# Attention loads paced by a 4-byte transfer, and the zero fills of expert 0's rows moved to later tiles

## The chip, the cores and the metric

The kernel runs on one core of a Trainium2 chip. The metric is device time in microseconds (us) for one execution, as the median of several runs. Beside the runs there is one profiled execution, and all rows of the trace below come from it; their times count from the first instruction of the span.

## The reference

Three layers follow each other on 2304 tokens (4 sequences of 576) of width 512. The first is a retention attention with 8 heads of 64, with no softmax: `scores = q k^T / 8`, multiplied by a decay mask, then `scores v`.

```
ret = scale * (q @ k^T) * Dmat          # Dmat = gamma_h ** (i - j) for i >= j, else 0
x = (ret @ v) laid out as 2304 x 512
noisy = x @ w_gate + log1p(exp(x @ w_noise)) * noise     # 8 experts, the best 2 per token
out[token] += weight * (relu(x[token] @ w1[e]) @ w2[e])  # F = 1024
h = out @ w_in;  g = h * clip(h + 3, 0, 6) / 6;  result = g @ w_out   # 2048 wide
```

## The kernel before

The work is written in one fixed order, and each engine runs its own part of it as an in-order queue. The attention stage takes 18 tiles of 128 tokens. Tile t needs three loads of 256 KB each (`load`, line 190: k, q, v), which SyncE's queue (SP) issues. VectorE scales k (`ks`, line 195) and q (`qs`, line 200), TensorE transposes k (`tr`) and multiplies (`qk`, line 225), and VectorE multiplies the scores by the mask into the tile `pt` (line 227, two instructions per tile). `av` and `av2` then use `pt` (lines 239 and 249), `kv` updates the running state (line 281).

In iteration t of the loop in `attention` (line 470) the program first issues `load(t + 3)`, for t from 1 to 14, and in four of the iterations (`WL`) a load of expert weights (`w_load`, lines 557 and 559). Then come, for the tile before, the row form of x (`xt`, evicted by ScalarE at line 295 into a buffer of the pool `row`) and `zero(t - 1)`; then `tr(t + 2)`, `av(t)`, `av2(t)`, `kv(t)`, `ks(t + 3)`, `qs(t + 3)` and `qk(t + 1)`. Tiles 0 to 3 are loaded ahead of the loop. k, q, v, `pt` and the weights share a pool of 32 buffers (`big`), handed out in turn as older ones come free; the program's order and these buffers are all that holds a load back.

After every third tile the router (`route`) works in small steps through the next two iterations and gives each token of the three tiles two slots in the DRAM array `xe`, one region per expert. `send` then scatters rows: GpSimd (POOL) first copies or clears a 4-byte `spacer` (lines 413 and 411), which waits for the engine that just produced a given tile, and then issues an indirect DMA of 128 rows of 2 KB (line 414). There are three sends in an iteration while slots are waiting: six scatters for a group of three tiles. Scatters are declared not to depend on each other. The groups are called 1 to 6 here; the scatters of group 1 are scatter 1 to 6.

`zero` writes 128 rows of zeros (`self.warm`, a buffer of the pool `row`) into expert 0's region, so that rows that no token fills are defined. The four fills cover rows 0 to 128, 128 to 256, 232 to 360 and 488 to 616. The framework orders any two DMAs that write overlapping parts of `xe`, and a scatter counts as writing all of it.

In iteration 14 (`GA`) the program sends all that is left of the first 12 tiles (four groups, 24 scatters) and issues `x_load(0, 0)` (line 670), three loads of expert 0's rows from `xe` behind these scatters, and behind them a 4-byte transfer into the DRAM word `paced` (line 514). These rows are turned at line 704, in the last iteration, and feed the first expert. The pool `row` has 13 buffers, of which the first four are `warm`, two state tiles and a table.

Of the kernel before, what the change touches and what calls it, by code (L numbers as in the profile page):

```python
# [19 lines left out]
NT = N // 128  # L20
RA, RB = 120, 128
NA, NB = 3 * RA, 2 * RB
CAP = NA + NB
# [10 lines left out]
P = 128  # L34
# [44 lines left out]
class K:  # L79
# [90 lines left out]

    def zero(self, j):

        if j < 4:
            r = (P, 2 * P, NA, CAP)[j]
            self.nc.gpsimd.dma_start(self.xe[r - P:r], self.warm.bitcast(F32))

    def load(self, t, names="kqv"):
# [36 lines left out]
    def qk(self, t):  # L214
        nc = self.nc
        r = self.raw[t]
        mk = C_MM if t % 9 == 4 else C_MK
        mask = self.c[:, mk:mk + P]
        pt = self.big([P, 2, 4, P])
        p0 = self.ps.tile([P, 4, P], F32, name="sc0", tag="ga")  # L220
        p1 = self.ps.tile([P, 4, P], F32, name="sc1", tag="gb")
        for a in range(4):
            for s, p in enumerate((p0, p1)):
                h = slice(s * 64, s * 64 + 64)
                nc.tensor.matmul(p[:, a, :], r["kT"][h, a, :], r["qT"][h, a, :], start=True, stop=True)  # L225
        for s, p in enumerate((p0, p1)):
            nc.vector.tensor_mul(pt[:, s], p, mask[:, None, :].to_broadcast([P, 4, P]))
        r["pt"] = pt
# [210 lines left out]
        yield  # L439

    def attention(self):
        self.raw, self.xrow, self.sq = {}, {}, []
        self.consts()
        self.load(0, "kq")
        self.load(1, "kq")
        self.nc.sync.dma_start(self.c[:, C_MK:], self.i["cst"][:, C_MK:C_W])
        self.load(0, "v")
        self.load(2, "kq")
        self.load(1, "v")
        self.load(3, "kq")  # L450
        self.load(2, "v")
        self.load(3, "v")
        self.busy(BZ[0])
        self.table()
        self.ks(0)
        self.tr(0)
        self.qs(0)
        self.ks(1)
        self.qs(1)
        self.busy(BZ[1])  # L460
        self.qk(0)
        self.gate_w()
        self.tr(1)
        self.ks(2)
        self.qs(2)
        self.late_consts()
        groups = [(g, 3) for g in range(0, NT, 3)]
        assert EARLY in [g[0] for g in groups]
        self.live, self.sent, self.xg = [], 0, {}
        for t in range(NT):  # L470
            if 0 < t < NT - 3:
                self.load(t + 3)
            if t in WL:
                self.w_load()
            self.rstep()

            if t:
                self.xt(t - 1)
                self.zero(t - 1)
            if 0 < t < NT - 2:  # L480
                self.tr(t + 2)
            if t and t % 3 == 0:
                self.gate(t - 1, groups)
            self.rstep()
            self.av(t)
            self.rstep()
            self.wstep(WM)

            self.av2(t)
            self.kv(t)  # L490
            if t == 0:
                self.tr(2)
            if t + 1 == NT:
                xs = self.x_new(0)
                self.x_tile(0, xs, 0, "acc")
                self.x_tile(0, xs, 1, "gb")
            self.rstep()
            if t + 3 < NT:
                self.ks(t + 3)
                self.qs(t + 3)  # L500

            if t + 1 < NT:
                self.qk(t + 1)
            if t % 3 == 2 and t + 1 < NT:
                self.gsum(t // 3)
            if t + 1 < NT:
                self.rstep()
            if t == GA:
                while self.sent < EARLY:
                    self.rstep()  # L510
                    self.send()
                self.xr = {}
                self.x_load(0, 0)
                self.nc.sync.dma_start(self.paced, self.xr[0, 0, 2][0:1, 0:1])
            if t in WS:
                self.w_split()
            if t + 1 < NT:
                self.wstep(WN)
        self.gsum(NT // 3 - 1)
        self.x_tile(0, xs, 2, "tp")  # L520
        self.xt(NT - 1)
        self.gate(NT - 1, groups)
        self.rstep()
        self.wstep(WN)
        return xs
# [913 lines left out]
```

## Time and profile before

| | |
|---|---|
| Median of 3 runs | 935.56 us (934.23 to 936.85) |
| Profiled execution, its own time | 936.64 us |
| Its span, first to last instruction | 934.5 us, so 2.14 us lie around it |
| TensorE busy | 921.8 us, 99% of the span |
| VectorE, ScalarE, GpSimd busy | 606.8, 466.5 and 235.9 us |
| Granted TensorE clock, mean | 0.998 |
| DMA | 221.22 MB, 237 GB/s over the span |

PE is the matmul side of TensorE and PEld its weight-load side; DVE is VectorE, ACT ScalarE, POOL GpSimd, SPq the queue of SyncE. Ends of matmuls are modelled, so a gap is easier to see on PEld than on PE. A "DMA share" is the mean busy share of the core's 16 DMA engines in a stretch; packets in flight overlap, so it can read slightly above 1. Brackets behind a row give the idle time of the engine before it, and what ended it.

### The profile page before, as it was taken

To read this page: it belongs to the slowest core of one execution; us is meant where nothing else is said; L and a number is where in the kernel's file an instruction comes from. 1 tells how busy PE (TensorE), PEld (TensorE's weight loads), DVE (VectorE), ACT (ScalarE), POOL (GpSimd) and SP (SyncE) were. 2 spreads that over 40 slices of the span, in tenths; PEclk is the share of its full clock that TensorE was granted. 3 is DMA by queue.
4 is the path that set the end of the run, shared out by engine and by line. 5 is a ranking of instruction groups with operands and counts; after the bars stand their busy time and mean duration, and the time that the engine had idled before them with its cause. 6 is when DMAs were issued, how large, how long until landed. Compare 5 with 4: busy or idle time off the path is not lost.

```text
span 934.5 us, 17789 instructions
## 1 busy us (share of the span) xinstructions
PE 921.8 (99%) x6314; PEld 818.2 (88%) x6314; DVE 606.8 (65%) x1327; ACT 466.5 (50%) x1025; POOL 235.9 (25%) x324
## 2 busy tenths in 40 slices
PE   9999999999999999999999999999999999999996
PEld 6887888988988889888888899999889998999985
DVE  5787747878879797787847446545745554564442
ACT  4666435455564645545544445544554464455432
POOL 1345531324233242432400221042004113300000
PEclk9999999999999999999999999999999999999999
DMA  9964877859879688896636787877578676846541
GB/s 339 386 243 147 304 243 232 238 187 280 259 241 282 227 256 271 248 267 218 224 111 214 265 298 252 307 247 240 188 262 270 205 258 227 271 166 228 167 150 49
DMA packets 123742, 221.22 MB, mean 237 GB/s; under 512 B 13037, under 2 KB 60915, under 8 KB 123643
## 3 DMA queue, kind: packets, MB, share of 16 engines
q1 hardware_dynamic: 113819, 190.47, 61.9%
q0 software_dynamic: 9392, 28.73, 9.1%
q8 instruction: 52, 0.85, 0.4%
q10 hardware_dynamic: 432, 0.79, 0.2%
q14 instruction: 47, 0.39, 0.1%
HBM read 163.97 MB, written 55.97 MB: 235 GB/s over the span
## 4 chain that ended last, share of the span: by engine, by line
PE 86%; DVE 7%; DMA 3%; issue 1%; ACT 1%; POOL 1%; SPq 0%; DVEq 0%; ACTq 0%; POOLq 0%
PE p L754 39%; PE ga L737 12%; PE gb L737 9%; PE mga L1168 7%; PE p L1168 5%; PE mgb L1168 2%; PE mtp L1168 2%; PE sc L225 2%; DVE b L591 1%; PE px L249 1%; PE p L293 1%; DVE cvt L635 1%; PE p L209 1%; DMA xe<-s,free 1%; DVE h L796 1%
## 5 line engine op out<-in xcount | busy, mean ns | idle before, releaser
L754 PE MATMUL p<-b,h 128*120 128x512 f32 (+1 forms) x1056 | 260.9, 395 | 0.0
L754 PEld LDWEIGHTS p<-b,h 128*120 128x120 f32 (+1 forms) x1056 | 189.2, 185 | 41.4 <-DVE h L796 0.4
L754 PE MATMUL p<-b,b 128*128 128x512 f32 x768 | 180.0, 390 | 0.0
L754 PEld LDWEIGHTS p<-b,b 128*128 128x128 f32 x768 | 142.3, 188 | 28.2
L737 PE MATMUL ga<-x,b 128*128 128x360 f32 (+1 forms) x768 | 134.4, 324 | 2.9 <-DVE h L796 2.9
L737 PEld LDWEIGHTS ga<-x,b 128*128 128x128 f32 x768 | 124.6, 188 | 12.1 <-DVE h L796 7.7
L640 POOL TENSOR_TENSOR cvl<-cvl,cvs 128x256 f32<-128x256 f32 x64 | 50.3, 785 | 229.9 <-ACT cva L621 163.0
L591 DVE TENSOR_TENSOR b<-b,b 128x512 fp32r<-128x512 f32 x128 | 89.6, 734 | 13.2 <-ACT b L590 12.9
L737 PE MATMUL gb<-b,b 128*128 128x256 f32 x672 | 89.7, 283 | 0.0
L737 PEld LDWEIGHTS gb<-b,b 128*128 128x128 f32 x672 | 86.9, 190 | 1.2
L885 POOL DMA_INDIRECT s<-yd,slotc x36 | 36.4, 1011 | 166.9 <-DVE x L991 48.4
L590 ACT ACTIVATE b<-b 128x512 fp32r<-128x512 f32 x128 | 74.1, 626 | 0.0
L1206 DVE SCALAR_TENSOR_TENSOR b<-s,b 128x512 fp32r<-128x512 f32 x64 | 44.3, 693 | 44.9 <-ACT b L1205 42.0
L1205 ACT ACTIVATE b<-s 128x512 fp32r<-128x512 f32 x64 | 40.5, 632 | 59.3 <-DVE s L1203 56.8
L796 DVE SCALAR_TENSOR_TENSOR h<-gb,h 128x256 fp32r<-128x256 f32 (+1 forms) x64 | 27.7, 433 | 50.2 <-PE p L754 35.2
L641 POOL TENSOR_TENSOR cvl<-cvt,cvl 128x256 f32<-128x256 f32 x64 | 58.2, 909 | 5.0
L1202 ACT ACTIVATE s<-s,three 128x512 f32<-128x512 f32 x64 | 45.9, 717 | 24.8 <-DVE s L1189 23.2
L1168 PE MATMUL mga<-b,b 128*128 128x256 f32 x384 | 56.3, 283 | 0.0
L1189 DVE TENSOR_TENSOR s<-p,mc 128x256 f32<-128x256 f32 x32 | 13.6, 424 | 65.4 <-PE p L1168 60.1
L1168 PEld LDWEIGHTS mga<-b,b 128*128 128x128 f32 x384 | 52.6, 191 | 2.5
L1203 DVE SCALAR_TENSOR_TENSOR s<-s,s 128x512 f32<-128x512 f32 x64 | 44.0, 687 | 7.5 <-DMA paced<-s 4.9
L1173 ACT ACTIVATE mc<-mga 128x256 f32<-128x256 f32 x64 | 24.6, 384 | 48.2 <-PE mga L1168 48.0
(206 smaller groups left out, 1433.6 us busy)
## 6 DMA issues: line engine op xcount, KB each, us to landing
b<-wc SPq DMA_DIRECT2D x112, 512.0 KB
b<-in_moe_w_dram SPq DMA_DIRECT2D x64, 512.0 KB
wc<-b SPq DMA_DIRECT2D x32, 512.0 KB
s<-xe SPq DMA_DIRECT2D x140, 64.0 KB
s<-in_moe_w_in_dram SPq DMA_DIRECT2D x32, 256.0 KB
s<-in_moe_w_out_dram SPq DMA_DIRECT2D x32, 256.0 KB
b<-wc SPq DMA_DIRECT2D x32, 256.0 KB
yd<-s SPq DMA_DIRECT2D x24, 240.0 KB
```

The costliest lines, as they stand in the source:

```text
L590: self.nc.scalar.activation(h, a, AF.Copy)
L591: rest = lambda h=h, l=l, a=a: self.nc.vector.tensor_sub(l, a, h.bitcast(F32))
L640: nc.gpsimd.tensor_mul(lf, lf, s.bitcast(F32))
L641: nc.gpsimd.tensor_add(lf, t.bitcast(F32), lf)
L737: nc.tensor.matmul(p, a[k], b[:, k, :n], start=(i == 0), stop=(i == 11))
L754: nc.tensor.matmul(a[:R], x[:, c], y[:, fi, :], start=(first and i == 0), stop=(last and i == 2))
L796: nc.vector.scalar_tensor_tensor(hl, p, 0.0, hh.bitcast(F32), op0=OP.max, op1=OP.subtract)
L1168: nc.tensor.matmul(t, w[:, u, k], x[:, z, k], start=(first and i == 0), stop=(last and i == 5), skip_group_check=True)
L1202: nc.scalar.activation(r, x, AF.Relu, bias=self.three)
L1203: v.scalar_tensor_tensor(x, r, 6.0, x, op0=OP.min, op1=OP.mult)
L1205: nc.scalar.activation(h[:, 0], x, AF.Copy, scale=1.0 / 6.0)
L1206: v.scalar_tensor_tensor(h[:, 1], x, 1.0 / 6.0, h[:, 0].bitcast(F32), op0=OP.mult, op1=OP.subtract)
```

## The change

Two things are changed. First, from iteration 3 on, a transfer of 4 bytes from the tile `pt` of tile t - 1 to the DRAM word `paced` is put into SP's queue ahead of `load(t + 3)`. It can only be issued once VectorE has written that part of `pt`. Each `qk(t)` for t from 2 to 13 keeps its `pt` for it. Second, `zero` does its four fills for j = 3, 4, 5, 6 in place of 0, 1, 2, 3, that is in iterations 4 to 7 in place of 1 to 4; the rows of the four fills and their order are the same.

```diff
     def zero(self, j):
 
-        if j < 4:
-            r = (P, 2 * P, NA, CAP)[j]
+        if 2 < j < 7:
+            r = (P, 2 * P, NA, CAP)[j - 3]
             self.nc.gpsimd.dma_start(self.xe[r - P:r], self.warm.bitcast(F32))
...
         pt = self.big([P, 2, 4, P])
+        if 1 < t < NT - 4:
+            self.pts[t] = pt
...
-        self.raw, self.xrow, self.sq = {}, {}, []
+        self.raw, self.xrow, self.sq, self.pts = {}, {}, [], {}
...
             if 0 < t < NT - 3:
+                if t > 2:
+                    self.nc.sync.dma_start(self.paced, self.pts.pop(t - 1)[0:1, 0, 0, 0:1])
                 self.load(t + 3)
```

## Rows read from the trace of the kernel before

**Rows 1.** The page, part 1: busy us, share of the span, instructions
```profile
PE 921.8 (99%) x6314; PEld 818.2 (88%) x6314; DVE 606.8 (65%) x1327; ACT 466.5 (50%) x1025; POOL 235.9 (25%) x324
```

**Rows 2.** Windows of 10 us: engines' busy time, clock, DMA share, GB/s
```profile
50.00:60.00 10.00, 10.00 (x161) 8.51 (x158) 8.12 (x32) 6.08 (x19) 7.29 (x11) 1.00 0.97 355
60.00:70.00 10.00, 10.00 (x162) 8.46 (x160) 9.21 (x26) 7.62 (x22) 3.74 (x6) 1.00 0.21 81
```

**Rows 3.** Waits from 0 to 95 us: total, times, longest
```profile
DVE b L195 <- DMA b<-in_k_dram: 2.6, 1, 2.6
```

**Rows 4.** Timeline of DVE, 0 to 79 us: start, duration, instruction
```profile
4.04 0.69 DVE L195 TENSOR_TENSOR b<-b,cst 128x512 f32<-128x512 f32 x1 [2.62 <-DMA b<-in_k_dram]
...
18.07 1.29 DVE L227 TENSOR_TENSOR b<-sc,cst 128x512 f32<-128x512 f32 x2 [1.48 <-PE sc L225]
...
42.14 1.29 DVE L227 TENSOR_TENSOR b<-sc,cst 128x512 f32<-128x512 f32 x2 [0.39 <-PE sc L225]
...
46.72 1.27 DVE L227 TENSOR_TENSOR b<-sc,cst 128x512 f32<-128x512 f32 x2
...
69.94 1.28 DVE L227 TENSOR_TENSOR b<-sc,cst 128x512 f32<-128x512 f32 x2
...
74.47 1.28 DVE L227 TENSOR_TENSOR b<-sc,cst 128x512 f32<-128x512 f32 x2
...
76.90 0.68 DVE L195 TENSOR_TENSOR b<-b,cst 128x512 f32<-128x512 f32 x1
```

**Rows 5.** Timeline of SP's queue, 0 to 150 us: issue time and duration
```profile
1.21 0.42 SPq L190 DMA_DIRECT2D b<-in_k_dram  x1
...
12.24 0.33 SPq L190 DMA_DIRECT2D b<-in_k_dram  x1
...
87.97 1.37 SPq L670 DMA_DIRECT2D s<-xe  x3
92.84 0.22 SPq L514 DMA_DIRECT2D paced<-s  x1
```

**Rows 6.** Waits of SP's queue from 0 to 135 us
```profile
SPq L670 <- DMA xe<-s,slots: 51.9, 2, 33.8
```

**Rows 7.** Timeline of PEld, 90 to 95 us
```profile
91.50 0.41 PEld L704 LDWEIGHTS p<-cst,s 120*128 120x128 f32 x4 [0.17 <-PE px L249]
...
93.58 0.41 PEld L704 LDWEIGHTS xp<-cst,s 120*128 120x128 f32 x4 [0.62 <-issue]
```

**Rows 8.** Timeline of POOL, 0 to 135 us
```profile
8.52 1.08 POOL L175 DMA_DIRECT2D xe<-s  x2
15.98 1.07 POOL L175 DMA_DIRECT2D xe<-s  x2 [6.38 <-DMA xe<-s]
...
39.38 1.00 POOL L414 DMA_INDIRECT xe<-s,slots  x1 [0.52 <-ACT b L211]
...
45.47 0.98 POOL L414 DMA_INDIRECT xe<-s,slots  x1 [0.15 <-issue]
...
67.07 0.30 POOL L413 COPY spacer<-s 1x1 f32<-1x1 f32 x1 [1.88 <-ACT s L295]
...
77.42 0.20 POOL L413 COPY spacer<-x 1x1 f32<-1x1 f32 x1 [2.02 <-ACT x L266]
```

**Rows 9.** Instructions on xe, windows 36:42, 57:60, 78:81: issue to landing
```profile
DMA to landing us min/median/max: 6.3/6.3/6.3
...
L414 POOL DMA_INDIRECT xe<-s,slots x3: 976/976/982, 56.1 to 58.8; - x3
...
DMA to landing us min/median/max: 3.4/3.4/3.5
...
DMA to landing us min/median/max: 2.7/2.7/2.7
```

**Rows 10.** Timeline of ACT, 54 to 77 us
```profile
59.70 1.17 ACT L590 ACTIVATE b<-b 128x512 fp32r<-128x512 f32 x2
...
66.35 0.59 ACT L295 ACTIVATE s<-p 128x512 f32<-128x512 f32 x1
```

## Prediction

> **What bounds the kernel now.** I read the page first. TensorE is busy for 99% of the span, and its weight-load side for 88% [rows 1]. So a change pays only if it takes idle time away from TensorE, and it costs only if it puts some in. The edits lie in the attention stage, the first 95 us. The windows there show the other extreme: the DMA share is 0.97 from 50 to 60 us and falls to 0.21 from 60 to 70 [rows 2]. The loads run far ahead, keep the DMA engines full, and are then over. The waits of this stage say whether anyone suffers: of the 18 tiles, one wait of VectorE for a load is there, 2.6 us for the very first k [rows 3]. No engine waits for a load after it.
>
> Does a full DMA slow TensorE or VectorE in some other way? The mask multiplications (line 227) of two tiles with the same place in the router's pattern of three are the test: tile 7 to tile 8 takes 46.72 - 42.14 = 4.58 us, with the DMA engines full; tile 13 to tile 14 takes 74.47 - 69.94 = 4.53 us, with the loads over [rows 4]. The 0.05 us between them is all that a full DMA could cost a tile. Over the some ten tiles that run while it is full that is 0.5 us.
>
> So of the transfers in this stage only the last is near the bound: `x_load(0, 0)`. SP issues its three loads from 87.97 us and passes their landing at 92.84 [rows 5], having waited up to 33.8 us for scatters [rows 6]. TensorE uses the first two tiles from 91.50 us, straight behind its own work (0.17 us idle), and the third from 93.58 [rows 7]. The third has 93.58 - 92.84 = 0.74 us to spare.
>
> **The loads, held back.** Without the change SP issues k of tile 6 at 12.24 us [rows 5]. With it, SP first waits for `pt` of tile 2, whose first half is written 0.65 us into the pair that starts at 18.07 [rows 4]: 18.72. So the edit binds, and it binds for all twelve held tiles, 6 to 17. What is late next? Take tile 17, one of the three with the least room. Its gate, half of the pair that starts at 69.94, opens at 70.58; its k is scaled at 76.90 [rows 4], so there are 6.32 us. SP needs 0.22 us for the 4-byte transfer (the one it has at line 514). A 256 KB load that starts with little ahead of it takes 4.04 - 1.21 = 2.83 us from issue to its user [rows 4, 5]. Together 3.05 us: 3.27 us to spare. The upper bound for a load is a 256 KB transfer in a full queue: the second fill was issued at 8.52 + 0.54 = 9.06, and its wait ended at 15.98 [rows 8], so 6.92 us. Then k would be 7.14 - 6.32 = 0.82 us late, at three tiles at most 2.5 us in all; the other nine have 7.3 us or more by the same reckoning. I take 2.83, because the held loads meet queues that are no longer full: 0.79 MB for each 4.72 us of a tile ((69.94 - 18.07) / 11 [rows 4]) is 167 GB/s, against 355 when they are full [rows 2]. Cost: nothing, between 0 and 2.5 us.
>
> The twelve added transfers cost SP 12 x 0.22 = 2.6 us, and SP waits for 33.8 us in one piece behind them. Queued behind each wait are one tile's loads and in some iterations expert weights. The first weights come behind tile 12, whose gate opens at 46.72 + 0.64 = 47.4. They are issued some 2.5 us later; 1 MB at 355 GB/s takes 3 us more than the 2.83, so they are there by 56. ScalarE first splits them at 59.70 [rows 10]. Cost: nothing.
>
> The Trainium skill, "DMA: Bandwidth & Descriptors", section "Rules for kernel authors", tells one to issue a DMA early and wait for it late, which is the opposite of this edit. By that rule the lead is what hides a transfer; the rows above put the lead needed at about 3 us, and 6.3 us are left.
>
> **The zero fills.** Here the change does not do what its place in the program suggests. POOL has nothing to wait for ahead of the first two fills, so they stay at 8.52 us, one right behind the other [rows 8]. The third and fourth, sent at 15.98 in the kernel before, now stand in POOL's queue behind scatter 2 and scatter 5. They write to `xe`, so each waits until those scatters have landed; and the scatter behind each waits until the fill has landed. These are four new waits on POOL. Queued behind them are the scatters of all later groups, and behind these `x_load` on SP and the row buffers that ScalarE's line 295 fills.
>
> I work the queue out with 3.4 us for each wait, what a scatter of 256 KB took while the queue was draining [rows 9]. Scatter 2 starts at 39.38 [rows 8] and lands at 42.8. The third fill lands at 46.2. Scatters 3, 4 and 5 start from there at a step of 1.35 us ((58.8 - 56.1) / 2 [rows 9]), the last at 48.9, landing at 52.3. The fourth fill lands at 55.7, and scatter 6 ends at 56.7, where it ended at 45.47 + 0.98 = 46.45 before [rows 8]: 10.2 us late. In short, scatter 6 ends at 39.38 + 2.70 + 0.98 + the four waits = 43.1 + the four waits.
>
> What takes this up is POOL's idle time, because sends are spaced by the tiles. The six scatters of group 2 now take 56.7 to 64.8. Group 3's first takes until 66.2, and its second is held until 67.07 anyway, where POOL sat idle for 1.88 us [rows 8]. From there the queue is as before, and group 4 starts at 77.42. Cost: nothing.
>
> The bounds are known. The four waits may be 2.7 us each, 10.8 in sum (a scatter at a quiet time [rows 9]), or two of 6.3 [rows 9] and two of 6.92, 26.4 in sum (both with full queues). Group 4 starts late once scatter 6 ends later than 77.42 - 12 x 1.35 = 61.2, which is a sum of 18.1 us, 4.5 each. With 26.4, `x_load` is 8.3 us late, of which 0.7 are to spare: 7.6 us on TensorE. I take 3.4 because the first edit empties the queues in exactly this stretch: 167 GB/s of loads, and some 90 of scatters and fills (six times 262 KB in 17 us), is well under 355.
>
> The row buffers give the same answer. `warm` is now read until 55.7 us; as buffers are handed out in the order in which they come free, its buffer goes to the row form of tile 11, which ScalarE writes at 66.35 [rows 10]. With full queues it is late by about 2 us; this is inside the 7.6.
>
> The Trainium skill, same page, section "Anatomy of one DMA — SWDGE (gpsimd) path", puts a DMA issued by GpSimd at 2.0 us plus bytes over 436 GB/s: an estimate of 2.6 us for 256 KB. The quiet 2.7 us agree with it, the 6.3 do not. By the page the four waits are 10.4 us, and nothing reaches `x_load`.
>
> **The sum** is 0 us on TensorE's path. The profiled execution would stay at 936.64 (934.5 + 2.14). The median shown is 1.08 us below it, so I give 935.6.
>
> **The rivals.**
>
> *A: the fills hold POOL up long enough to delay `x_load`* (slower). For it: four waits that did not exist, and 6.3 and 6.9 us were seen in full queues. The first weights come at 49 to 53 us, just when scatter 5 and the fourth fill have to land. Against it: the draining queue of the stretch. It decides from a sum of 18.1 us. Full queues throughout give 935.6 + 7.6 = 943; a sum of 20 gives 1.2 us and could not be told from nothing.
>
> *B: the held loads come late*, and VectorE stalls at line 195. It decides from a load of 6.1 us, and even at 6.92 it costs at most 2.5 us: 938.1. Against it: 2.83 us [rows 4, 5]. This is the way in which the Trainium skill's rule of early issue, named above, would have it go.
>
> *C: emptier queues help* (faster). The one lever with a row is the 0.05 us a tile, 0.5 us in all: 935.1. A gain over 0.3% would need a wait that no view shows.
>
> *D: the pacing is too loose to bind.* It is ruled out above: the gate opens at 18.72, the load went at 12.24.
>
> **How the numbers follow.** 0.3% is 2.8 us, about what a measurement of this kernel can tell from no change. The forecast has 0.78, A 0.12, B 0.03, C 0.07. Of A, sums up to 21.6 us stay within 0.3% (0.7 to spare and 2.8 on top): I put 0.03 there and 0.09 above. B stays within it. Of C, 0.02 stays within. So faster 0.05, same 0.86, slower 0.09. The forecast's own range is the spread of the runs before, 934.2 to 936.9. For eight in ten I reach up into A and B, to 938.5, and a little below the runs for C, to 933.8.
>
> **What the next profile would show.** If the steps are right: k of tile 6 issued at about 19 us and of tile 17 at about 71; the DMA share from 20 to 60 us well below 1 and from 60 to 70 above 0.21; two fills still at 8.5 us, the third at 42 to 44, the fourth at 51 to 54; scatter 6 ending at 55 to 59; group 4's first copy still near 77.4, `x_load` near 88, no wait of VectorE for a load but the first. The prediction is wrong if group 4 starts later than 79 us, if line 195 or line 295 waits for DMAs, or if TensorE's tile takes clearly less than 4.5 us.

## The result, and the profile after

The changed kernel takes 945.0 us (median of 4 runs, 940.43 to 946.79) against 935.38 us: a ratio of 1.0093, with a 95% interval of 1.0076 to 1.0109. It is slower by some 9 us. The forecast was no change, 935.6 us, in a range of 933.8 to 938.5; the time lies above it, near rival A's 943. The profiled execution is the shortest of the four (940.43 us, span 938.2), so its waits may well be shorter than those of the median run.

TensorE stays busy for 99% of a longer span, 2.8 us longer than before; the other engines' busy times moved by 1.6 us at most against [rows 1].

```profile
PE 924.6 (99%) x6314; PEld 819.8 (87%) x6314; DVE 607.8 (65%) x1327; ACT 466.9 (50%) x1025; POOL 236.5 (25%) x324
```

The windows of 10 us after the change (engines' busy time, clock, DMA share, GB/s) answer to [rows 2]. The full DMA engines have moved, from the time before 60 us to the time after it: the first row below is of the kernel before, the others are of the changed one. From 50 to 60 us the share is still 0.90, where the prediction looked for "well below 1". In the last window TensorE's busy time falls, and so does its granted clock.

```profile
70.00:80.00 10.00, 10.00 (x165) 7.89 (x164) 9.09 (x35) 6.13 (x21) 6.74 (x11) 1.00 0.31 120
...
40.00:50.00 10.00, 10.00 (x179) 8.77 (x175) 9.20 (x37) 6.19 (x20) 3.83 (x7) 1.00 0.64 214
50.00:60.00 10.00, 10.00 (x161) 8.51 (x158) 7.94 (x32) 6.08 (x19) 2.03 (x3) 1.00 0.90 305
60.00:70.00 10.00, 9.99 (x159) 8.21 (x158) 9.21 (x25) 7.65 (x22) 5.32 (x8) 1.00 1.01 360
70.00:80.00 10.00, 10.00 (x163) 7.83 (x162) 7.00 (x31) 5.76 (x20) 8.86 (x15) 1.00 1.03 380
80.00:90.00 10.00, 8.34 (x103) 6.90 (x101) 5.79 (x14) 6.17 (x15) 8.49 (x15) 0.83 0.67 262
```

POOL's timeline after, beside [rows 8]: two fills still at 8.4 us, then scatter 2, the third fill, scatters 3 and 5, the fourth fill, scatter 6, and the first copy of group 4, which is 5.46 us later than 77.42.

```profile
8.42 1.08 POOL L175 DMA_DIRECT2D xe<-s  x2
...
39.39 1.00 POOL L416 DMA_INDIRECT xe<-s,slots  x1 [0.51 <-issue]
42.96 0.59 POOL L175 DMA_DIRECT2D xe<-s  x1 [2.57 <-DMA xe<-s,slots]
...
47.02 1.00 POOL L416 DMA_INDIRECT xe<-s,slots  x1 [3.29 <-ACT s L285]
...
50.02 1.26 POOL L416 DMA_INDIRECT xe<-s,slots  x1 [0.16 <-issue]
58.39 0.59 POOL L175 DMA_DIRECT2D xe<-s  x1 [7.11 <-DMA b<-in_moe_w_dram]
...
64.21 1.32 POOL L416 DMA_INDIRECT xe<-s,slots  x1 [5.05 <-ACT s L285]
...
82.88 0.21 POOL L415 COPY spacer<-x 1x1 f32<-1x1 f32 x1
```

The releasers in brackets are the last semaphore events seen, not always the true ones (ScalarE has nothing to do with scatter 3); the place in the queue tells what is waited for. The four waits are 42.96 - 39.39 = 3.57, 47.02 - 42.96 = 4.06, 58.39 - 50.02 = 8.37 and 64.21 - 58.39 = 5.82 us: 21.8 us in sum.

SP's queue after (issue times), beside [rows 5]: k of tile 6 and k of tile 17 stand where they were forecast, at 19 and 71 us; the first weights go out at 49.13; `x_load` starts 4.85 us later than 87.97.

```profile
19.14 0.35 SPq L190 DMA_DIRECT2D b<-in_k_dram  x1
...
49.13 0.47 SPq L561 DMA_DIRECT2D b<-in_moe_w_dram  x1
...
71.36 0.34 SPq L190 DMA_DIRECT2D b<-in_k_dram  x1
92.82 1.31 SPq L674 DMA_DIRECT2D s<-xe  x3
97.66 0.22 SPq L518 DMA_DIRECT2D paced<-s  x1
```

The waits of the first 100 us after, beside [rows 3], name two engines that stand still for a DMA: VectorE for k (three times in place of once, 3.6 us the longest) and ScalarE for a row buffer that a late scatter still reads.

```profile
DVE b L195 <- DMA b<-in_k_dram: 6.4, 3, 3.6
...
ACT s L297 <- DMA xe<-s,slots: 3.7, 2, 2.8
```

On TensorE's weight-load side the late k of tile 17 shows as 1.66 us of idle at 81.81. Then the 16 loads of `qk` take 1.26 us where the next tile's take 0.97: the granted clock was 0.57 from 84 to 88 us. The use of expert 0's rows (95.93) comes 4.4 us later than 91.50 in [rows 7], but TensorE waits only 0.19 us for it: at the last tile's `av` (the first row below is of the kernel before, the second of the changed one) it was already 93.11 - 88.76 = 4.35 us late. So in this shortest run the stall for k, with the slower clock behind it, runs beside the lateness of `x_load` and hides it.

```profile
88.76 0.14 PEld L239 LDWEIGHTS px<-b,s 64*64 64x64 f32 x2 [0.17 <-issue]
...
93.11 0.14 PEld L241 LDWEIGHTS px<-b,s 64*64 64x64 f32 x2 [0.17 <-issue]
```

```profile
81.81 0.42 PEld L209 LDWEIGHTS p<-cst,b 128*128 128x128 f32 x4 [1.66 <-issue]
...
87.05 1.26 PEld L227 LDWEIGHTS sc<-b 64*128 64x128 f32 x16
...
91.43 0.97 PEld L227 LDWEIGHTS sc<-b 64*128 64x128 f32 x16
...
95.93 0.41 PEld L708 LDWEIGHTS p<-cst,s 120*128 120x128 f32 x4 [0.19 <-PE px L251]
```

### The profile page after: what moved, and what is told of

Read it like the earlier page. It is cut to its first block, busy times and chain, and to the rows that moved or that the text cites. A ratio compares the mean times of both kernels' runs of the same rounds, so it can differ in the third digit from the quotient of the medians.

```text
span 938.2 us, 17804 instructions
## 1 busy us (share of the span) xinstructions
PE 924.6 (99%) x6314; PEld 819.8 (87%) x6314; DVE 607.8 (65%) x1327; ACT 466.9 (50%) x1025; POOL 236.5 (25%) x324
## 4 chain that ended last, share of the span: by engine, by line
PE 86%; DVE 6%; DMA 3%; POOL 2%; issue 2%; ACT 1%; SPq 0%; DVEq 0%; ACTq 0%; POOLq 0%
PE p L758 39%; PE ga L741 12%; PE gb L741 9%; PE mga L1172 7%; PE p L1172 5%; PE mgb L1172 2%; PE mtp L1172 2%; PE sc L227 2%; DVE b L595 1%; PE px L251 1%; DVE cvt L639 1%; PE p L295 1%; POOL xe L416 1%; DVE h L800 1%; PE p L209 1%
## 5 line engine op out<-in xcount | busy, mean ns | idle before, releaser
L595 DVE TENSOR_TENSOR b<-b,b 128x512 fp32r<-128x512 f32 x128 | 89.7, 736 | 12.5 <-ACT b L594 12.3
L1206 ACT ACTIVATE s<-s,three 128x512 f32<-128x512 f32 x64 | 45.9, 717 | 25.4 <-DVE s L1193 23.8
L1193 DVE TENSOR_TENSOR s<-p,mc 128x256 f32<-128x256 f32 x32 | 13.6, 425 | 65.0 <-PE p L1172 65.0
```

The costliest lines, as they stand in the source:

```text
L595: rest = lambda h=h, l=l, a=a: self.nc.vector.tensor_sub(l, a, h.bitcast(F32))
L1206: nc.scalar.activation(r, x, AF.Relu, bias=self.three)
```

## The experiments

Two theories stood against each other. Theory F: the late fills hold POOL. Theory L: the held loads come late by themselves. Each ratio below is against the kernel before on the same chip, with its 95% interval.

**The two parts alone, and a control.** First the pacing alone: the fills go back.

```diff
-        if 2 < j < 7:
-            r = (P, 2 * P, NA, CAP)[j - 3]
+        if j < 4:
+            r = (P, 2 * P, NA, CAP)[j]
```

> The loads are paced as in the change; the fills are back in iterations 1 to 4. Theory F (the two fills that now stand behind scatters hold POOL, the scatters come late and bunched, and x_load and the row buffers follow): with the fills early the scatters start as in the kernel before, group 4 at about 77.4 us, x_load at about 88, and the time is 934 to 937 us. Theory L (holding the loads moves tiles and expert weights into 50 to 80 us, where they come late by themselves): VectorE still waits some 3 us for k of tile 17, and the time stays at 939 to 945 us.

Measured: 936.77 us, 1.0017 (1.0008 to 1.0026). Both are partly right. Group 4 is on time, within 0.5 us. But k of tile 17 is late without the fills, by 2.61 us where the whole change has 3.62, in VectorE's timeline:

```profile
78.88 0.69 DVE L195 TENSOR_TENSOR b<-b,cst 128x512 f32<-128x512 f32 x1 [2.61 <-DMA b<-in_k_dram]
```

Then the fills alone: the same edit of `zero` as in the change, with no pacing.

> The fills are in iterations 4 to 7 as in the change; the loads run ahead as in the kernel before. Theory F: the four waits of POOL fall into full queues, 6.3 us for a scatter and 6.9 us for a fill, 26 us in sum; group 4 starts about 8 us late and the time is 940 to 944 us. Theory L: no load is held, so 934 to 937 us.

Measured: 938.61 us, 1.0041 (1.0028 to 1.0054). Theory F's sign, at less than the forecast size: the four waits were 18.1 us, not 26. The two parts add up to 0.6% where the change costs 0.9%.

The control sends the twelve transfers from a constant.

```diff
-                    self.nc.sync.dma_start(self.paced, self.pts.pop(t - 1)[0:1, 0, 0, 0:1])
+                    self.nc.sync.dma_start(self.paced, self.c[0:1, 0:1])
```

> The twelve 4-byte transfers are sent, but from a constant that has long landed, so they hold nothing back; the fills are early. Theories F and L both: 934 to 937 us, with loads issued as in the kernel before. A rival, that the transfers themselves cost (SP's time, or a place among the transfers in flight): 938 us or more.

Measured: 935.73 us, 0.9999 (0.9990 to 1.0008). With nothing held back the transfers cost nothing; the holding does.

**Waits or bytes.** Both kernels pace the loads and keep the four early fills. The first adds two fills of one row, ordered against the scatters; the second adds two full fills to a spare array, ordered against nothing.

```diff
+        if j in (5, 6):
+            r = (NA, CAP)[j - 5]
+            self.nc.gpsimd.dma_start(self.xe[r - 1:r], self.warm.bitcast(F32)[0:1])
```

> Paced loads, the four full fills early as in the kernel before, and in iterations 6 and 7 two more fills of one row each (2 KB), which have the places and the order against the scatters of the late fills, and almost no bytes. If POOL's waits for landings are what counts: scatter 3 and scatter 6 start late all the same, with 3 to 4 us a wait at the first pair and more at the second; group 4 starts 2 to 4 us late, 938 to 942 us. If the bytes of the late fills are what fills the queue: as the paced loads alone, 936 to 937.5 us.

```diff
+        if j in (5, 6):
+            self.nc.gpsimd.dma_start(self.spare[(j - 5) * P:(j - 4) * P], self.warm.bitcast(F32))
```

> Paced loads, the four fills early, and in iterations 6 and 7 two more full fills of 256 KB into a spare array, which overlap with no scatter. If POOL's waits count: nothing waits, group 4 starts as with the paced loads alone, 936 to 937.5 us. If the bytes count: 939 us or more.

This chip ran the kernel before in 948.06 us, so only ratios count: 1.0079 (1.0036 to 1.0122) for the waits without bytes, 0.9997 (0.9982 to 1.0012) for the bytes without waits. The order costs, and the bytes do not. POOL's timeline of the one-row fills: 4.10 and 4.49 us for the first pair of waits, 7.73 and 3.70 for the second, 20.0 in sum.

```profile
39.29 1.00 POOL L419 DMA_INDIRECT xe<-s,slots  x1 [0.51 <-issue]
...
43.39 0.56 POOL L178 DMA_DIRECT2D xe<-s  x1 [3.11 <-ACT s L300]
...
47.88 1.02 POOL L419 DMA_INDIRECT xe<-s,slots  x1 [3.72 <-ACT s L300]
...
50.94 0.98 POOL L419 DMA_INDIRECT xe<-s,slots  x1 [0.16 <-issue]
58.67 0.56 POOL L178 DMA_DIRECT2D xe<-s  x1 [6.74 <-DMA xe<-s,slots]
...
62.37 1.03 POOL L419 DMA_INDIRECT xe<-s,slots  x1 [2.98 <-ACT s L288]
```

And of the full fills to the spare array: the fill goes out right behind scatter 2, and scatter 3 right behind the fill.

```profile
39.39 1.00 POOL L419 DMA_INDIRECT xe<-s,slots  x1 [0.51 <-issue]
40.39 0.59 POOL L178 DMA_DIRECT2D spare<-s  x1
41.39 1.29 POOL L419 DMA_INDIRECT xe<-s,slots  x1 [0.16 <-ACT x L271]
```

By which path the order costs time on this chip is not seen. Group 4 starts 90.86 - 84.49 = 6.4 us later in the first kernel than in the second, but POOL had made up its waits by then and stood idle for 3.16 us until ScalarE had written the tile:

```profile
90.11 0.31 POOL L418 COPY spacer<-x 1x1 f32<-1x1 f32 x1 [3.16 <-ACT x L271]
```

**A longer lead.** Early fills, and the gate two tiles sooner.

```diff
-        if 1 < t < NT - 4:
+        if 1 < t < NT - 6:
...
-                if t > 2:
-                    self.nc.sync.dma_start(self.paced, self.pts.pop(t - 1)[0:1, 0, 0, 0:1])
+                if t > 4:
+                    self.nc.sync.dma_start(self.paced, self.pts.pop(t - 3)[0:1, 0, 0, 0:1])
```

> Early fills; each load of tile t + 3 is gated by the scores of tile t - 3 in place of t - 1, so two tiles sooner, from iteration 5 on. Theory L (k of tile 17 comes late because it is issued at 70 us behind weights and between scatters): it is issued at about 61 us, no wait of VectorE at line 195, 935 to 936 us. If pacing costs in another way (lost lead of the weights, order in the queue): 936.8 us as with a lead of four tiles.

On the 948 us chip: 1.0011 (0.9994 to 1.0028), and no wait of VectorE for a load behind the first tiles. The late loads are gone; whether that gives back the 0.17% is inside the interval.

**The change once more.**

> The change itself once more, beside the next three kernels on one chip. The first profile was of the shortest of its runs (940.4 us where the median was 945.0). If the rest of the cost is TensorE at its lower clock behind the waits: a profile with a longer time shows the same waits of a few us and a longer stretch at the lower clock, and over the runs the span grows as the mean granted clock falls. Ratio to the kernel before 1.007 to 1.011.

Measured: 944.85 us (median of five runs, 938.02 to 947.01), 1.0094 (1.0064 to 1.0124). This profile (943.68 us) is of a more typical run. POOL's four waits are 3.97, 6.59, 8.20 and 5.85 us, 24.6 in sum, and group 4's first scatter starts at 85.65:

```profile
38.49 0.99 POOL L416 DMA_INDIRECT xe<-s,slots  x1 [0.52 <-issue]
42.46 0.59 POOL L175 DMA_DIRECT2D xe<-s  x1 [2.97 <-ACT s L297]
49.05 1.36 POOL L416 DMA_INDIRECT xe<-s,slots  x1 [5.83 <-ACT x L268]
...
52.06 0.98 POOL L416 DMA_INDIRECT xe<-s,slots  x1 [0.16 <-issue]
60.26 0.59 POOL L175 DMA_DIRECT2D xe<-s  x1 [7.22 <-ACT b L594]
66.11 1.01 POOL L416 DMA_INDIRECT xe<-s,slots  x1 [4.87 <-DMA xe<-s]
...
85.65 0.99 POOL L416 DMA_INDIRECT xe<-s,slots  x1 [0.16 <-issue]
```

Now TensorE does wait for expert 0's rows, 4.30 us (its weight-load side), and the four loads behind the wait take 0.69 us where they took 0.41 in [rows 7]:

```profile
98.12 0.69 PEld L708 LDWEIGHTS p<-cst,s 120*128 120x128 f32 x4 [4.30 <-issue]
```

The windows of 2 us of this run show why: behind the idle time the granted clock (the third figure from the right) is 0.50, the 1.2 GHz level, until about 102 us.

```profile
94.00:96.00 2.00, 0.06 (x1) 0.00 (x0) 0.64 (x2) 0.00 (x0) 0.00 (x0) 0.87 0.20 78
96.00:98.00 2.00, 0.00 (x0) 0.00 (x0) 0.00 (x0) 0.00 (x0) 0.00 (x0) 0.50 0.92 246
98.00:100.00 2.00, 1.85 (x9) 1.57 (x10) 0.10 (x1) 0.57 (x1) 0.00 (x0) 0.50 0.53 123
100.00:102.00 2.00, 2.00 (x20) 0.74 (x19) 1.60 (x5) 0.70 (x2) 0.00 (x0) 0.50 0.25 56
102.00:104.00 2.00, 2.00 (x17) 2.00 (x17) 0.74 (x2) 1.44 (x3) 0.00 (x0) 0.92 0.93 315
```

The Trainium skill, "TensorE: Matmul & The Clock Gate", section "Part 1: The HAM clock gate (the 'warmup' mystery)", says that the array falls to its lower level when idle and comes back with work; this trace agrees (0.50 from 96 to 102 us, 0.92 in the next window).

**What the lower clock costs.** The kernel with both parts and early weights (a later paragraph) has one clean stall ahead of expert 0's rows. Six matmuls that no one reads are put into it:

```diff
+                p = self.pacc([P, 512])
+                for _ in range(6):
+                    self.nc.tensor.matmul(p[:, 0:384], self.ident, self.c[:, 0:384], start=True, stop=True)
                 xs = self.x_new(0)
```

> The kernel with both parts of the change and early weights (940.8 us), with six matmuls that no one reads put ahead of the first use of expert 0's rows, where TensorE stood idle for 4.3 us and then ran at the lower clock for 6.8 us. They take some 4 us of that wait. If the lower clock behind the wait is a part of the cost: it does not come, and the time falls by 2 to 3.5 us, to 937.3 to 938.8 us. If only the wait costs: 940.8 us, or a little more.

On the 948 us chip 1.0119 (1.0087 to 1.0152), without the kernel that lacks the six matmuls beside it; so both were run again together.

> Both parts of the change with the first three weight loads early, once more, as the kernel to which the fillers of the next one are compared on the same chip. TensorE idle for about 4 us ahead of expert 0's rows, no wait of VectorE for k of tile 17, ratio 1.005 to 1.009.

> The same with six unread matmuls ahead of the first use of expert 0's rows. On the earlier chip this gave 1.0119 with nothing beside it to compare. If the lower clock behind the wait is part of the cost, the stretch at half clock behind the first use is gone or shorter, and the ratio is lower than that of the kernel without them by 0.002 to 0.004. If the fillers cannot hold the clock up, or cost their own time, the ratio is the same or higher.

Measured on one chip: 943.73 us, 1.0087 (1.0072 to 1.0103) without the matmuls; 939.73 us, 1.0053 (1.0040 to 1.0066) with them. Added useless work takes 4.0 us off the median, though in the profiles group 4 started no earlier (1.4 us later, counted from scatter 2) and expert 0's rows landed no earlier (SP passes them at 96.68 us with the matmuls, at 96.55 without). Without them the clock is 0.50 from 96 to 104 us; the first row below is of that kernel, the others keep the full clock:

```profile
96.00:98.00 2.00, 2.00 (x21) 1.19 (x21) 1.12 (x2) 0.88 (x2) 0.00 (x0) 0.50 0.06 17
...
92.00:94.00 2.00, 2.00 (x8) 1.19 (x7) 0.00 (x0) 0.00 (x0) 0.00 (x0) 1.00 0.26 79
94.00:96.00 2.00, 1.90 (x9) 0.94 (x8) 0.00 (x0) 0.19 (x1) 0.00 (x0) 1.00 0.80 281
96.00:98.00 2.00, 2.00 (x27) 1.35 (x27) 1.48 (x4) 1.42 (x3) 0.00 (x0) 1.00 0.06 18
```

**What makes the waits long.** Weights early:

```diff
-WL, WS = (9, 11, 13, 15), (10, 14)
+WL, WS = (3, 5, 7, 15), (10, 14)
```

> Both parts of the change, but the first three expert weight loads are issued in iterations 3, 5 and 7 in place of 9, 11 and 13, so that their 3.1 MB no longer fall into 49 to 70 us. Theory F with the weights as what fills the queue: the four waits of POOL are 3.5 to 4.5 us each, 14 to 18 in sum, group 4 starts at most 1 us late, 935 to 937 us. Theory L says the same for k of tile 17: no wait of VectorE, 935 to 937 us. If the waits stay long without the weights (scatters and fills alone fill the queue): 939 us or more.

Measured: 940.79 us, 1.0068 (1.0050 to 1.0085). k of tile 17 is on time, but the waits are 21.3 us all the same: the first pair grew to 12.3 us, where the third weight load now went out at 38.8 us beside it, and the second shrank to 9.0. So the weights were kept away from both pairs, with `WL = (3, 5, 13, 15)`:

> Both parts of the change; the first three weight loads are issued in iterations 3, 5 and 13, so that none of their 1 MB lies beside either of the two late fills. A pair of POOL's waits took 7.6 and 8.0 us where no weights lay beside it and 12 to 14 us where they did. If the weights are what made the waits long: 15.6 us in sum, under the 18.1 us from which my prediction let it cost; group 4 starts at most 1.5 us late, no stretch at half clock before 900 us, and what is left is k of tile 17 (1.4 us in the paced loads alone): ratio 1.001 to 1.004. If tiles and scatters alone keep the waits over 18 us: 1.006 or more.

Measured: 939.81 us, 1.0052 (1.0039 to 1.0065): between the two forecasts. The pairs were 10.9 and 9.2 us, 20.1 in sum. Tiles and scatters alone keep them over the threshold, at 243 and 246 GB/s in the two stretches (39 to 50 and 52 to 62 us).

One late fill, the third, with the fourth early:

```diff
+        if j in (0, 1, 3, 5):
+            r = {0: P, 1: 2 * P, 3: CAP, 5: NA}[j]
```

> Paced loads; the third fill (rows 232 to 360) at its late place, behind scatter 2, the fourth early with the first two. So one pair of POOL's waits, 7 to 8 us, is left of two, 22 us. By the idle time of POOL that my prediction counted (some 14 us between the groups' sends) the pair is taken up: group 4 starts within 0.5 us of the paced loads alone, and the ratio is 1.000 to 1.003. If any late fill is enough: 1.005 or more.

Measured: 940.44 us, 1.0048 (1.0035 to 1.0061): missed as well. The pair took 10.1 us, and POOL had enough idle time to take it up. Still group 4's first copy came at 80.61 us, behind 3.59 us of idle POOL: the tile was late, not the queue. With POOL's earlier idle time gone the scatters follow each other without a pause, and VectorE waits for k twice (2.0 us) and for q three times (2.4 us), in the waits of 50 to 98 us. The pacing alone has 2.6 and 0.4 us there, so these 1.4 us more explain a part of the cost; the rest is open.

```profile
DVE b L200 <- DMA b<-in_q_dram: 2.4, 3, 1.1
DVE b L195 <- DMA b<-in_k_dram: 2.0, 2, 1.1
```

**Late loads taken away.** A lead of six tiles on top of `WL = (3, 5, 13, 15)`, and a lead of six in the change as it is:

> The same, and each load gated two tiles sooner (a lead of six). If late loads are the rest of the cost: no wait of VectorE at line 195 behind the first, ratio 0.999 to 1.002. If the late fills cost in a way that is neither POOL's waits nor late loads: 1.003 or more.

> The change with a lead of six tiles in place of four, and nothing else: weights come some 9 us sooner than in the change, beside the first pair of waits. Loads no longer late, but POOL's waits 18 to 24 us in sum: x_load 2 to 6 us late, ratio 1.004 to 1.008. If late loads are the larger part of the change's cost: 1.003 or less.

Measured: 943.14 us, 1.0072 (1.0060 to 1.0084), and 944.22 us, 1.0098 (1.0085 to 1.0111). No wait of VectorE for k or q is left in either from 50 to 102 us, and the time does not fall. Both expectations were too low. But POOL's waits were 24.3 us against 20.1 without the longer lead, and 23.8 against 21.8 and 24.6, so the two runs do not price late loads by themselves; the pacing alone does, 0.17%. They also show a second path of the late scatters, beside `x_load`: ScalarE waits 4.1 us for a row buffer that a scatter still reads, and TensorE some 2.6 us behind it, 11 us ahead of its wait for expert 0's rows (3.5 and 3.25 us). The granted clock falls to 0.50 behind each of the two stalls. Of the first kernel:

```profile
85.41 0.60 ACT L297 ACTIVATE s<-p 128x512 f32<-128x512 f32 x1 [4.10 <-DMA xe<-s,slots]
86.81 0.91 PEld L295 LDWEIGHTS p<-cst,x 128*128 128x128 f32 x4 [2.56 <-ACT x L268]
```

All profiles with two full late fills on the chips that run the kernel before in 935 us, side by side. The lateness is group 4's start counted from scatter 2, less the same in the kernel before (78.17 - 39.38 = 38.79 us).

| kernel | the two pairs of waits, us | sum | group 4 late by | sum - lateness |
|---|---|---|---|---|
| fills only | 11.3 + 6.9 | 18.1 | 2.0 | 16.2 |
| weights miss both pairs | 10.9 + 9.2 | 20.1 | 4.0 | 16.1 |
| early weights, again | 12.2 + 8.0 | 20.2 | 3.5 | 16.6 |
| early weights | 12.3 + 9.0 | 21.3 | 5.0 | 16.4 |
| early weights, fillers (again) | 12.5 + 9.2 | 21.7 | 4.9 | 16.8 |
| the change | 7.6 + 14.2 | 21.8 | 5.1 | 16.8 |
| lead of six, late fills | 12.6 + 11.2 | 23.8 | 7.6 | 16.2 |
| weights miss, lead of six | 11.0 + 13.3 | 24.3 | 7.6 | 16.7 |
| the change again | 10.6 + 14.1 | 24.6 | 8.4 | 16.2 |

In these nine every microsecond of the four waits above some 16.4 us is a microsecond on group 4. On the 948 us chip this does not hold: the early weights with fillers have 21.0 us and group 4 late by 10.9, the one-row fills 20.0 and 12.8, and the full fills without order, with none of these waits, are late by 6.3. There POOL stood idle ahead of group 4 (6.19 us in the first of them), so other delays come first; no profile of the kernel before was taken on that chip.

## Why the prediction was wrong

**What bounds the kernel, and the first edit.** The gates opened when and where they were worked out (k of tile 6 at 19.14 us, of tile 17 at 71.36), and the first weights were in time (split at 59.71). The control shows that the transfers are free while nothing is held. In the change one of them went out at 58.16 us, 2 us behind its gate, and SP's waits name the landing of the transfer before it, which goes to the same word; the sum had no such term. Wrong were the 2.83 us of a load and its upper bound too. The bound was 6.92 us, taken from one fill; k of tile 17 took from 71.36 to 81.00, 9.6 us. The pacing alone costs 0.17%, about 1.6 us, inside the 0 to 2.5 us that were given.

**The fills: the step that failed.** The path was right in every link: two fills do not move, two stand behind scatters 2 and 5, four new waits, then group 4, `x_load` and the row buffers. The step that failed is the size of one term: "I take 3.4 because the first edit empties the queues in exactly this stretch". The four waits were put at 13.6 us; they were 21.8 and 24.6, nearer to the upper bound of 26.4. The sum behind the step counted tiles, scatters and fills, at 257 GB/s. It left out that the first edit moves three weight loads of 1 MB as well, from 30 to 49 us to 49 to 70 (rival A names the first of them, and no term has it), and that scatters held back come out without pauses. From 60 to 80 us the DMA engines were as full as they had been before 60. In the table the weights show as some 3 us for a pair that has them beside it: in the eight profiles with paced loads, 11.2 to 14.2 us (12.8 on average) against 7.6 to 11.0 (9.4). But the larger error is in the reading of a mean rate as a landing time. Without weights a pair takes 9.4 us where 6.8 were taken, at rates below the 257 GB/s of the sum: 243 and 246 in the kernel whose weights miss both pairs. And from 40 to 50 us the change moved 214 GB/s in one profile and 208 in the other, and its first pair took 7.6 and 10.6 us. What exactly stretches a landing to 4 to 6 us with no weights near stays open; the bytes of the fill do not, since a one-row fill waits as long.

**The threshold** of 18.1 us came out at 16.4, mostly because the twelve scatters behind scatter 6 took steps of 1.47 to 1.55 us on average and not of 1.35. The slope of 1 above it held in the nine profiles of the table.

**Rival A** was the right mechanism, with too small a chance (0.12): in the second profile of the change and in those with early weights TensorE stands still for expert 0's rows. Its price, 7.6 us with full queues, is met by the change's second profile: group 4 late by 8.4 us, the span longer by 941.6 - 934.5 = 7.1. What it left out is the clock. A wait of TensorE of some 4 us is paid twice, once as idle time and once as the stretch at 1.2 GHz behind it; the fillers gave 4.0 us back. That can take the median beyond the 943 of full queues. In the first set of the change's runs the longest span, 944.7 us, has the lowest mean clock (0.991) and the shortest, 938.2, the highest (0.996). The second set shows this at its short end only (935.9 us at 0.999): 941.6, 944.6 and 944.9 us all have 0.995, so the clock does not explain the whole spread.

The row buffers were put "inside the 7.6", as late by about 2 us for `warm`. They were late by up to 2.8 us in the change and 4.1 with a lead of six, for the buffers of late scatters; there TensorE's stall for them comes on top of the one for `x_load`.

**Rivals B and C.** B exists, at 0.17%. C, a gain from emptier queues, did not come: the queues were not emptied, only filled later.

The Trainium skill, "DMA: Bandwidth & Descriptors", section "Issuing engines are not separate DMA queues", says that DMAs of all engines interleave on the same 16 DMA engines. The kernel with one late fill fits this: with POOL's scatters unspaced VectorE waits 4.4 us for SP's loads, against 3.0 in the pacing alone.

## What to carry to other kernels

A transfer that is held back is not taken away: list every load behind it in the same queue, and add up the stretch that they all move into before calling it empty. Even then a mean rate is not a landing time; take the landing from a row with the same traffic, or leave a range. An order between DMAs of one in-order queue costs a full landing each way, here with 2 KB as with 256 KB, so a fill belongs ahead of the first write that it must be ordered against. Idle time of a queue may be what spaces its traffic, and a stall of TensorE should be priced with the lower clock that can follow it.

## What the runs showed of the hardware

An ordered fill of 2 KB held POOL about as long as one of 256 KB: 20.0 us for four waits, against 21.0 with full late fills (and early weights) on the same chip, and 20.1 to 24.6 in the paced kernels on the others. A scatter of 256 KB landed in 2.7 us at a quiet time [rows 9] and in 8.1 us by the same view when it started at 50.02 us in the change. And useless matmuls in a stall of TensorE made a kernel 4.0 us faster.
